# A third score buffer, a later scaling and another last sweep in an attention and ReLU-square kernel on one core

## The chip, the cores and the metric

The kernel runs on one core of a Trainium2 chip. The metric is the time of one execution on the device in microseconds (us), median of the runs. Five engines work side by side, each with its own queue of instructions: TensorE (PE; its weight loads are shown as PEld), VectorE (DVE), ScalarE (ACT), GpSimd (POOL) and SyncE (SP, which issues the transfers). Matmul results go to eight banks (PSUM), which TensorE, DVE and ACT reach; GpSimd works on SBUF alone.

## The reference

Attention over 32 heads (4 x 8, length 1152, depth 64) with queries averaged in pairs, then a two-layer block with a squared ReLU:

```python
q_pool = q.reshape(B, H, S // 2, 2, D).mean(axis=3)
scores = (1 / sqrt(D)) * q_pool @ k.transpose(0, 1, 3, 2)
attn = exp(scores - max(scores)); attn = attn / (sum(attn) + 1e-09)
x = (attn @ v).transpose(0, 2, 1, 3).reshape(2304, 512)
r = maximum(x @ w_in, 0)                  # w_in: 512 x 2048
out = (s * (r * r) + b) @ w_out           # w_out: 2048 x 512
```

Inputs are float64 (the weights) and float32; the output is 2304 x 512 float32.

## The kernel before

Every float32 operand is split in a high part (of a shorter format that TensorE takes in one pass) and the rest, the low part. A product is three matmuls: high by high, high by low, low by high.

**Attention.** 288 steps (32 heads x 9 key tiles, the loop at L841). A step makes scores of one key tile (`score_step`, L686: four matmuls of 288 columns, two buffers `s` of two banks each), and the product with v of the tile three steps before (`value_step`, L714). In between stand products `m` for the row maxima of heads to come (`max_unit`, L621, two banks `m`); they run 15 steps ahead, so the last 15 steps have none. A step has a kind (`KIND`, L36): for `w` ScalarE takes one exponential and the product with v is made in float32 (four records of L724); for `v` and `g` it takes two exponentials, one of them rounded, the difference `pl` is made by DVE from the score bank (`v`) or by GpSimd from a copy in SBUF (`g`), and the product with v is six matmuls (L730 to L734). When a pair of heads ends, `finish` (L739) queues by steps (`XT`, L44) two transposes and a reciprocal on DVE, a product on GpSimd (`scale`) and the DMA of the result (`send`).

**First and second sweep.** The hidden columns are 16 groups of 128. Groups 0 to 2, then 3 to 7, are worked for nine blocks of 256 rows. A unit is `mm1` (L355: 12 matmuls into a bank `h`, three buffers) and, four units later, `mm2` (L382). Between lies a chain: ReLU (ACT), square (DVE), `image` (ACT), `rest` (DVE, writes `gl` at L374 and is the last to read the bank). `later(k, fn)` issues an instruction k steps later; `pace` (L922) makes a step and, every seven steps, starts the conversion of one piece of weights.

**Last sweep** (groups 8 to 15, from L957). Two groups are one pair n, and two blocks one s. Unit (s, n) computes a 2 x 2 product of blocks with seven instead of eight block products: `first_half` (b11, t1, t3, t2; 24 matmuls) and `second_half` (b21, t4, b22; 18). Its results go to four quarters of two banks `xy0` and `xy1`, each with two buffers; b11 and t2 are the halves of one bank. ScalarE copies b11 (`one`, L1219), DVE adds it to t2 (`kept`, L1223) and so on; L1229 and L1232 write the results into ring tiles `rr`. n = 0, and block 8, are made with plain products (`plain`, L411). The second layer is also made with seven products per pair and block (`pair2`, L444, 21 matmuls into four banks `seven`), after additions on the operand (`prepare`, L1265: `one`, `two`, `three`, `own_high`, `own_low`, `high`, `low`). `gather` (L1317) adds the four banks of a block to the earlier part of the output, nine additions (L1331), and sends it (L1362).

The order of TensorE in this sweep is written out (`order`, L970 to L997; `TAKE` says how many pairs stand between the parts of the units). All other instructions are placed by a planner: each `op` has costs by engine, what it comes after, and beats of TensorE by which it must be done (`need`, `require`); from these it has a latest time, moved forward by `EARLY`. The loop at L1463 takes, among what can start within `LOOK` of the soonest, the most urgent; `BIAS` says how much longer an operation may take on GpSimd than on DVE (L1492 to L1499):

```python
            if at > soon + LOOK:
                continue
            if any(e2 != e and o2 is o and end2 < end - BIAS for _, end2, e2, o2, _ in choice if o2 is o):
                continue
```

Of the kernel before, what the change touches and what calls it, by code (L numbers as in the profile page):

```python
# [43 lines left out]
XT = (2, 2, 4, 4, 8)  # L44
SW = (3, 8)
# [20 lines left out]
def attention_moe_kernel(ctx: ExitStack, tc: tile.TileContext, q, k, v, w_in, w_out, s_in, b_in, out):  # L66
# [246 lines left out]
    class Moe:  # L313


        def __init__(self):
            self.acc = {}
            self.x, self.g, self.yq, self.y, self.raw, self.done = {}, {}, {}, {}, {}, []
            self.begun = 0

# [33 lines left out]
        def mm1(self, blk, f):  # L354
            xh, xl = self.x[blk]  # L355
            h = self.hp.tile([P, 512], F32, tag="h", name=f"h{blk}_{f}")
            n = 0
            for c in range(NC):
                for st, mv in ((wi_hi[f], xh), (wi_hi[f], xl), (wi_lo[f], xh)):
                    nc.tensor.matmul(h[:, :TB], st[:, c, :], mv[:, c, :], start=(n == 0), stop=(n == 3 * NC - 1))  # L360
                    n += 1
            r = self.p.tile([P, TB], F32, tag="r", bufs=2, name=f"r{blk}_{f}")
            t = h[:, TB:]
            gh = self.p.tile([P, TB], F32R, tag="gh", bufs=DEPTH + 1, name=f"gh{blk}_{f}")
            gl = self.p.tile([P, TB], F32R, tag="gl", bufs=DEPTH + 1, name=f"gl{blk}_{f}")

            def square():
                nc.vector.scalar_tensor_tensor(out=t, in0=h[:, :TB], scalar=sb[:, 0:1], in1=r, op0=ALU.mult, op1=ALU.mult)

            def image():  # L370
                nc.scalar.activation(gh, t, AF.Identity, bias=sb[:, 1:2])

            def rest():
                nc.vector.scalar_tensor_tensor(out=gl, in0=t, scalar=sb[:, 1:2], in1=f32(gh), op0=ALU.add, op1=ALU.subtract)  # L374
                self.g[blk, f] = gh, gl

            nc.scalar.activation(r, h[:, :TB], AF.Relu)
            for at, fn in zip(MO, (square, image, rest)):
                later(at, fn)
# [31 lines left out]
        def plain(self, blk, n):  # L411
            f0 = SW[1] + 2 * n
            own = blk == NBLK - 1
            h = self.bank[blk, n] = self.hp.tile([P, 512], F32, tag="h" if own else f"xy{blk % 2}", bufs=3 if own else 2, name=f"h{blk}_{f0}")
            if own:
                x = [[t[:, c] for t in self.x[blk]] for c in (slice(0, NC // 2), slice(NC // 2, NC))]
            else:
                x = [self.x[blk // 2, name] for name in (("b11", "b21"), ("b12", "b22"))[blk % 2]]
            for e in range(2):
                w = wi_hi[f0 + e], wi_lo[f0 + e]  # L420
                for half in range(2):
                    c = slice(half * NC // 2, (half + 1) * NC // 2)
                    self.product(h[:, e * TB:(e + 1) * TB], [t[:, c] for t in w], x[half], half == 0, half == 1)
                    yield

        def first_half(self, s, n):
            f0 = SW[1] + 2 * n
            xy = self.bank[s, n] = [self.hp.tile([P, 512], F32, tag=f"xy{e}", bufs=2, name=f"xy{e}_{s}_{n}") for e in range(2)]
            quad = [t[:, e * TB:(e + 1) * TB] for t in xy[::-1] for e in range(2)]
            w11 = tuple(t[f0][:, :NC // 2] for t in (wi_hi, wi_lo))  # L430
            for to, w, name in ((quad[2], w11, "b11"), (quad[0], self.s[n][0], "t1"), (quad[1], self.s[n][2], "t3"), (quad[3], self.s[n][1], "t2")):
                self.product(to, w, self.x[s, name], True, True)
                yield

        def second_half(self, s, n):
            f0 = SW[1] + 2 * n
            quad = [t[:, e * TB:(e + 1) * TB] for t in self.bank[s, n][::-1] for e in range(2)]
# [5 lines left out]
        def pair2(self, blk, n):  # L443
            first, last = n == 0, n == (NF - SW[1]) // 2 - 1  # L444
# [11 lines left out]

        def start(self, blk):
            self.y[blk] = [self.yp.tile([P, 512], F32, tag="y", name=f"y{blk}_{i}") for i in range(TB // P)]
# [7 lines left out]
    ps_m = att.enter_context(tc.tile_pool(name="ps_m", bufs=2, space=PSUM))  # L466
    ps_o = att.enter_context(tc.tile_pool(name="ps_o", bufs=1, space=PSUM))

# [215 lines left out]
    fresh = []  # L684

    def score_step(hd, j, kind):  # L686
# [52 lines left out]
    def finish(hd, a):  # L739
# [101 lines left out]
    for n in range(NS + LAG):  # L841
# [5 lines left out]
        for part in ORDS.get(n % 18, ORD[at]) if at is not None else "sff":  # L847
            if part == "s" and n < NS:
                score_step(hd, j, KIND[n % 18])
# [69 lines left out]
    wait = 0  # L919
# [63 lines left out]
    for s in range(NSB):  # L983
# [6 lines left out]
        for n in range(NP):  # L990
            if n not in PLAIN[s]:
                order.append(("first", (s, n)))
                for _ in range(1 if i else 2):
                    between(s, i)
                    i += 1
                order.append(("half", (s, n)))
    order += [("pair", e) for e in range(k, len(slots))]  # L997
    length = {"plain": (.716,) * 4, "second": (.693,) * 2, "banks": (), "first": (.716,) * 4, "half": (.716,) * 3, "pair": (.716, .716, .716, .358)}
# [29 lines left out]
    for (kind, i), b in begin.items():  # L1028
# [3 lines left out]
        elif kind == "first":  # L1032
            for e, name in enumerate(("b11", "t1", "t3", "t2")):
# [79 lines left out]
    def sums(s, n, at, old):  # L1113
# [45 lines left out]
        l1 = op(low(both(1), lambda: w[1], both(0)), E(512), h1, need=begin["first", (s, n)] + 1)  # L1159
# [27 lines left out]
    def image(key, tile, after):  # L1187
# [4 lines left out]
        made[key] = op(fn, A(.53), *after)  # L1192
# [17 lines left out]
    def unit(s, n, banks):  # L1210
# [3 lines left out]
        quad = lambda i: moe.bank[s, n][1 - i // 2][:, i % 2 * TB:(i % 2 + 1) * TB]  # L1214
        wide = lambda: moe.bank[s, n][1].rearrange("p (e t) -> p e t", t=TB)
# [18 lines left out]
        o1 = op(first, A(.32), b, *(one_by[-2:-1]), need=b + 3)  # L1234
# [23 lines left out]
        require(b, *banks[0])  # L1258
        require(b + 1, *banks[1])
        return [(c1,), (d,)]  # L1260
# [4 lines left out]
    def prepare(k, blk, n):  # L1265
        b = begin["pair", k]
# [33 lines left out]
        new = {}  # L1300
        new["one"] = op(one, VP(256), done, was(1, "one"), was(2, "low"))
# [15 lines left out]
    def gather(k, blk, end, before):  # L1317
        p = begin["pair", k]
        first = begin["pair", k - NP + 1]
# [39 lines left out]
        drained[:] = [aa, bb, *a1, *b2], [ma, m0], [z]  # L1359

# [3 lines left out]
        s0 = op(send(0), SY(2.5), aa, bb, *a1, ma, m0)  # L1364
        s1 = op(send(1), SY(2.5), aa, bb, *b2, ma, z)
# [41 lines left out]
    banks_of = [[(mults[-2],), (mults[-1],)], [(mults[-2],), (mults[-1],)]]  # L1407
    for s in range(NSB):
        for e in range(2):
            for n in PLAIN[s]:  # L1410
                q = plain(2 * s + e, n, banks_of[e][-2])
                banks_of[e].append((q,))
        for n in range(NP):
            if n not in PLAIN[s]:
                a, b = unit(s, n, (banks_of[0][-2], banks_of[1][-2]))
                banks_of[0].append(a)
                banks_of[1].append(b)
# [5 lines left out]
    drained[:] = [[kept_y[0][0], kept_y[1][0], mults[-1]], [], []]  # L1423
    for k, (blk, n) in enumerate(slots):
        if n == NP - 1:
            end = k == len(slots) - 1
            if end:
                drained[:] = [[x for e in range(2) for y in banks_of[e][-2:] for x in y], [], []]
# [34 lines left out]
    while waiting or beat_n < len(beats):  # L1463
# [26 lines left out]
        soon = min(x[0] for x in choice)  # L1490
        best = None
        for at, end, e, o, locked in choice:  # L1492
            if at > soon + LOOK:
                continue
            if any(e2 != e and o2 is o and end2 < end - BIAS for _, end2, e2, o2, _ in choice if o2 is o):
                continue
            key = limit[o["n"]] - (end - at)
            if best is None or key < best[0]:
                best = key, at, end, e, o, locked  # L1499
        if best is None:  # L1500
            at, end, e, o, locked = min((x for x in choice), key=lambda x: x[1])
        else:
            _, at, end, e, o, locked = best
# [9 lines left out]
    def products():  # L1513
        for kind, i in order:
# [9 lines left out]
            elif kind == "banks":  # L1524
                banks.close()
                moe.hp = ctx.enter_context(tc.tile_pool(name="ps_h3", reuse_waits="tile", bufs=2, space=PSUM))
                ps_7 = ctx.enter_context(tc.tile_pool(name="ps_7", reuse_waits="tile", bufs=1, space=PSUM))
                moe.hp.tile([P, 512], F32, tag="xy1", bufs=2, name="spare")
                moe.seven = [ps_7.tile([P, 512], F32, name=f"seven{i}") for i in range(4)]
            elif kind == "first":  # L1530
                yield from moe.first_half(*i)
            elif kind == "half":
                yield from moe.second_half(*i)
            else:
                blk, n = slots[i]
                if i == len(slots) - NP:
                    moe.seven = [moe.hp.tile([P, 512], F32, tag=f"xy{e}", bufs=2, name=f"last{e}_{x}") for e in range(2) for x in range(2)]
# [41 lines left out]
```

## Time and profile before

| | |
|---|---|
| Runs | 895.52, 895.66, 895.93 us (median 895.66) |
| The profiled execution | 895.35 us, of which the span of instructions is 893.6 us |
| PE busy | 871.8 us (98%), 6028 matmuls |
| PEld busy | 825.5 us (92%) |
| DVE busy | 741.5 us (83%) |
| ACT busy | 619.5 us (69%) |
| POOL busy | 656.4 us (73%) |
| granted TensorE clock | 0.999 of full speed |

The busy time of an engine is the time covered by at least one of its instructions. A matmul's end is modelled, and matmuls overlap: the distance from one start to the next tells what one costs, and a longer distance is a wait. The attention runs from 0 to about 493 us, the first two sweeps to about 693 us, the last sweep to the end.

### The profile page before, as it was taken

The numbers are of one execution on the slowest core, as the hardware profiler recorded it, in microseconds if no ns is written. First come the engines' busy times: TensorE is split into PE (matmuls) and PEld (weight loads), VectorE is DVE, ScalarE is ACT, GpSimd is POOL, SyncE is SP. The second block draws the span as 40 slices with busy tenths as digits, with TensorE's granted clock in tenths as the row PEclk, the third lists the DMA queues.
The fourth block names the chain that finished last, engine by engine and source line by source line (L and its number), as shares of the span: only waits on it lengthen the run. The fifth ranks groups of instructions, "written<-read, shape, count | busy, mean of one in ns | idle before, by whom it ended". The sixth has DMA issues, their size and how long they took to land.

```text
span 893.6 us, 17383 instructions
## 1 busy us (share of the span) xinstructions
PE 871.8 (98%) x6028; PEld 825.5 (92%) x6028; DVE 741.5 (83%) x1367; ACT 619.5 (69%) x1162; POOL 656.4 (73%) x576
## 2 busy tenths in 40 slices
PE   5999999999999999999999999999999999999997
PEld 3899999999999999999998899989999999999997
DVE  5888888888888888888874788789884999999977
ACT  3777777878777777778778677766663656656543
POOL 7978877988898889888957567579985365744523
PEclk9999999999999999999999999999999999999999
DMA  9899788887988898879553566766642212231112
GB/s 160 160 180 191 162 163 173 165 182 161 178 165 173 169 179 160 181 165 184 134 138 98 160 197 207 220 198 212 189 142 87 95 33 68 75 95 48 49 71 72
DMA packets 255207, 130.42 MB, mean 146 GB/s; under 512 B 203728, under 2 KB 226896, under 8 KB 255120
## 3 DMA queue, kind: packets, MB, share of 16 engines
q1 hardware_dynamic: 248016, 128.43, 60.9%
q10 hardware_dynamic: 7104, 0.89, 0.7%
q8 instruction: 48, 0.79, 0.4%
q14 instruction: 39, 0.32, 0.1%
HBM read 68.16 MB, written 18.87 MB: 97 GB/s over the span
## 4 chain that ended last, share of the span: by engine, by line
PE 82%; DVE 11%; ACT 3%; issue 1%; DMA 1%; SPq 1%; POOL 0%; ACTq 0%; DVEq 0%; POOLq 0%
PE s L692 17%; PE h L360 11%; PE y L387 10%; PE m L637 8%; PE o L724 7%; PE o L734 6%; PE o L732 6%; PE o L730 6%; PE seven L453 6%; PE xy L408 4%; DVE yq L1331 2%; DVE pm L638 1%; DVE c L1276 1%; DMA qraw<-in_q_dram 1%; PE h L408 1%
## 5 line engine op out<-in xcount | busy, mean ns | idle before, releaser
L638 DVE TENSOR_REDUCE pm<-m 128x1 f32<-128x384 f32 x432 | 226.2, 546 | 45.7 <-PE m L637 42.2
L692 PE MATMUL s<-qq,kk 128*128 128x288 f32 x1152 | 207.8, 302 | 1.7 <-DVE qq L666 1.3
L701 ACT ACTIVATE ph<-s 128x576 fp32r<-128x576 f32 x224 | 146.0, 652 | 79.7 <-PE s L692 76.1
L692 PEld LDWEIGHTS s<-qq,kk 128*128 128x128 f32 x1152 | 174.1, 189 | 10.6 <-issue 2.5
L707 POOL TENSOR_TENSOR pl<-pe,ph 128x576 fp32r<-128x576 f32 x96 | 138.5, 1455 | 50.9 <-ACT pe L704 50.8
L637 PE MATMUL m<-kh,qz 128*128 128x384 f32 x384 | 137.6, 378 | 0.2
L734 PE MATMUL o<-pl,vv 128*128 128x288 f32 x448 | 132.1, 295 | 0.0
L732 PE MATMUL o<-ph,vl 128*128 128x288 f32 (+1 forms) x448 | 132.0, 295 | 0.0
L730 PE MATMUL o<-ph,vv 128*128 128x288 f32 x448 | 131.6, 294 | 0.0
L707 DVE TENSOR_TENSOR pl<-s,ph 128x576 fp32r<-128x576 f32 x128 | 96.5, 754 | 28.8 <-ACT s L704 26.9
L360 PE MATMUL h<-x,wih 128*128 128x256 f32 x576 | 106.7, 283 | 1.1 <-DVE gl L374 1.0
L360 PEld LDWEIGHTS h<-x,wih 128*128 128x128 f32 x576 | 93.7, 190 | 7.9 <-DVE gl L374 2.1
L734 PEld LDWEIGHTS o<-pl,vv 128*128 128x128 f32 x448 | 84.2, 188 | 3.0
L730 PEld LDWEIGHTS o<-ph,vv 128*128 128x128 f32 x448 | 84.1, 188 | 0.0
L704 ACT ACTIVATE s<-s 128x576 f32<-128x576 f32 x128 | 83.2, 650 | 0.0
L360 PE MATMUL h<-x,wil 128*128 128x256 f32 x288 | 81.6, 283 | 0.0
L637 PEld LDWEIGHTS m<-kh,qz 128*128 128x128 f32 x384 | 73.4, 194 | 6.6 <-DVE pm L638 2.7
L724 PE MATMUL o<-pe,vf 128*128 128x288 f32 x256 | 77.4, 405 | 0.0
L732 PEld LDWEIGHTS o<-ph,vl 128*128 128x128 f32 (+1 forms) x448 | 73.8, 165 | 0.0
L1279 POOL TENSOR_TENSOR c<-rr 128x128 f32<-128x128 f32 x36 | 24.8, 690 | 54.3 <-ACT rr L1190 31.5
L704 ACT ACTIVATE pe<-s 128x576 f32<-128x576 f32 x96 | 61.9, 644 | 0.0
L387 PE MATMUL y<-woh,gh 128*128 128x512 f32 x144 | 56.9, 395 | 0.0
(428 smaller groups left out, 2329.5 us busy)
## 6 DMA issues: line engine op xcount, KB each, us to landing
kk<-kh SPq DMA_DIRECT2D x31, 576.0 KB, 5.6
vf<-in_v_dram SPq DMA_DIRECT2D x32, 288.0 KB, 4.3
qq<-qh SPq DMA_DIRECT2D x64, 144.0 KB, 5.7
kk<-kT SPq DMA_DIRECT2D x31, 288.0 KB, 3.3
xr<-xd SPq DMA_DIRECT2D x17, 512.0 KB, 4.0
qraw<-in_q_dram SPq DMA_DIRECT2D x120, 72.0 KB, 2.6
kraw<-in_k_dram SPq DMA_DIRECT2D x60, 144.0 KB, 3.5
wsti<-in_moe_w_in_dram SPq DMA_DIRECT2D x13, 512.0 KB, 4.0
```

The costliest lines, as they stand in the source:

```text
L360: nc.tensor.matmul(h[:, :TB], st[:, c, :], mv[:, c, :], start=(n == 0), stop=(n == 3 * NC - 1))
L387: nc.tensor.matmul(y[:, :DM], st[:, ts_], mv, start=(first and n == 0), stop=(last and n == 2))
L637: nc.tensor.matmul(ps[:, :KB], st, khs[p][:, e * KB:(e + 1) * KB], start=True, stop=True)
L638: nc.vector.tensor_reduce(out=pms[p][:, col, e:e + 1], in_=ps[:, :KB], axis=AX.X, op=ALU.max)
L692: nc.tensor.matmul(ps[:, a, :HALF], kk[:, i, j * P:(j + 1) * P], qq[:, i, a], start=(i == 0), stop=(i == 1))
L701: nc.scalar.activation(ph, ps[:, :, :HALF], AF.Exp, scale=SCALE)
L704: nc.scalar.activation(full, ps[:, :, :HALF], AF.Exp, scale=SCALE)
L707: fresh.append(lambda: eng.tensor_tensor(out=pl, in0=full, in1=f32(ph), op=ALU.subtract))
L724: nc.tensor.matmul(o[:, :HALF], vfs[hd % 2][:, j], ph[:, a], start=first, stop=last)
L730: nc.tensor.matmul(o[:, :HALF], vv[:, j], ph[:, a], start=first, stop=False)
L732: nc.tensor.matmul(o[0:vl.shape[2], :HALF], vl[:, j], ph[:, a], start=False, stop=False)
L734: nc.tensor.matmul(o[:, :HALF], vv[:, j], pl[:, a], start=False, stop=last)
```

## The change

- Attention: kinds of the last 18 steps from `KINDL` (three w, twelve v, three g; before four, eight, six). The pool of the maxima is opened last and closed after the step by which all maxima have begun; its two banks become a third score buffer, taken by every third step.
- `XL`: for the last pair of heads transposes, reciprocal, scaling and DMA are issued 16 steps later. `MF`: in the first four units of the first sweep `rest` is issued after 4 steps, not 6. `W0`: the conversion of weights for the last groups begins 6 steps later.
- Last sweep: a unit has a bank `y` (t1, t3; two buffers, shared with `plain`) and banks `xa` (b11) and `xb` (t2) of one buffer each; the order in the first half is t1, t3, b11, t2. `TAKE` puts pairs elsewhere, 28 in all before the last eight, as before. The rings have 4 and 5 tiles for 3 and 3. `EARLY`, `LOOK`, `BIAS` and the choice differ: DVE is taken only where it ends first, GpSimd where it ends at most `BIAS` after that.
- The last pair (`tail`): instead of 21 matmuls 24 plain ones, in four groups of six, each group's half bank in the banks of the block before. The sums for the seven products are then made once over three pairs while the plain ones run, and four single additions follow, one after each group.

```diff
+XL = 16
+KINDL = "wvwvvgvvgvvwvvgvvv"
+MF = (2, 3, 4)
+W0 = 6
-RR = (3, 3)
+RR = (4, 5)
-TAKE = ((0, 1, 1, 1, 1), (1, 1, 2, 2, 2))
+TAKE = ((0, 0, 1, 0, 1, 0, 2, 0), (0, 2, 2, 0, 2, 0, 2, 0))
-LOOK, BIAS = 0.1, 0.33
-EARLY = {"sums": 1, "image": 2, "unit": -0.5, "gather": 1, "fetch_raw": -2}
+LOOK, BIAS = 0.3, 0.62
+EARLY = {"keep": 2, "unit": 0.1, "fetch_raw": 2, "plain": 0.1, "sums": 0.1, "image": 2}
...
-            for at, fn in zip(MO, (square, image, rest)):
+            for at, fn in zip(MO if len(self.turns) > DEPTH else MF, (square, image, rest)):
...
-            xy = self.bank[s, n] = [self.hp.tile([P, 512], F32, tag=f"xy{e}", bufs=2, name=f"xy{e}_{s}_{n}") for e in range(2)]
-            quad = [t[:, e * TB:(e + 1) * TB] for t in xy[::-1] for e in range(2)]
+            y, x0, x1 = self.bank[s, n] = [self.hp.tile([P, 512], F32, tag=tag, bufs=bufs, name=f"{tag}{s}_{n}") for tag, bufs in (("y", 2), ("xa", 1), ("xb", 1))]
+            quad = [y[:, :TB], y[:, TB:], x0[:, :TB], x1[:, :TB]]
...
-            for to, w, name in ((quad[2], w11, "b11"), (quad[0], self.s[n][0], "t1"), (quad[1], self.s[n][2], "t3"), (quad[3], self.s[n][1], "t2")):
+            for to, w, name in ((quad[0], self.s[n][0], "t1"), (quad[1], self.s[n][2], "t3"), (quad[2], w11, "b11"), (quad[3], self.s[n][1], "t2")):
...
+        def tail(self, blk, n):
+            own, both = self.g.pop((blk, n))
+            _, w1r, d1, d2, w0l, _, _ = seven[n]
+            for i in range(2):
+                g0, g1 = [[t[:, (2 * e + i) * P:(2 * e + i + 1) * P] for t in own] for e in range(2)]
+                c = [t[:, i] for t in both]
+                for half, todo in enumerate((((c, w0l), (g1, d2)), ((g0, d1), (c, w1r)))):
+                    y = self.seven[2 * i + half][:, :HD]
...
-        ps = ps_s.tile([P, 2, 512], F32, tag="s", name=f"s{hd}_{j}")
+        if third and (hd * NJ + j - third[0]) % 3 == 2:
+            ps = third[1].tile([P, 2, 512], F32, tag="t", name=f"s{hd}_{j}")
+        else:
+            ps = ps_s.tile([P, 2, 512], F32, tag="s", name=f"s{hd}_{j}")
...
-                later(at, fn)
+                later(at + (XL if p == NPAIR - 1 else 0), fn)
...
+        if not third and begun(n + 1) == NPAIR * NU:
+            maxima.close()
+            third.extend((n + 1, att.enter_context(tc.tile_pool(name="ps_t", bufs=1, space=PSUM))))
...
-    wait = 0
+    wait = W0
...
-        made[key] = op(fn, A(.53), *after)
+        made[key] = op(fn, A(.71), *after)
...
-        o1 = op(first, A(.32), b, *(one_by[-2:-1]), need=b + 3)
+        o1 = op(first, A(.32), b + 2, *(one_by[-2:-1]), need=h)
...
-        require(b, *banks[0])
-        require(b + 1, *banks[1])
-        return [(c1,), (d,)]
+        require(b, *banks[2])
+        require(b + 2, *banks[0])
+        require(b + 3, *banks[1])
+        return (c0,), (c1,), (d,)
...
+        if end:
+            t0 = begin["tail", k + 1]
+            rows = [[op(add(single(2 * i + e), lambda at=2 * i + e: moe.sums[at][:, :HD]), V(.34), got, t0 + 2 * i + e) for e in range(2)] for i in range(2)]
...
-            for e, (c, locked) in o["costs"].items():
-                at = max(t, idle[e], port if locked is True else 0.)
-                choice.append((at, at + c, e, o, locked))
...
+            at = {e: max(t, idle[e], port if locked is True else 0.) for e, (c, locked) in o["costs"].items()}
+            ends = {e: at[e] + o["costs"][e][0] for e in at}
+            choice += [(at[e], ends[e], e, o, o["costs"][e][1]) for e in at if ends[e] <= min(ends.values()) + (BIAS if e == "G" else 0.)]
+        soon = min(x[0] for x in choice) + LOOK
+        at, end, e, o, locked = min((x for x in choice if x[0] <= soon), key=lambda x: limit[x[3]["n"]] - x[1] + x[0])
```

## Rows read from the trace of the kernel before

**Rows 1.** The page's first line: the span.

```profile
span 893.6 us, 17383 instructions
```

**Rows 2.** Busy time by stage: stretch, length, then each engine (instructions), clock, DMA.

```profile
461.00:492.80 31.80, 31.43 (x210) 28.88 (x210) 16.04 (x27) 26.57 (x48) 24.25 (x20) 1.00 0.36 93
492.80:693.00 200.20, 199.11 (x1274) 180.16 (x1273) 154.93 (x292) 129.64 (x276) 144.26 (x114) 1.00 0.58 181
693.00:866.90 173.90, 171.58 (x1406) 169.41 (x1406) 158.92 (x285) 103.52 (x184) 88.33 (x90) 1.00 0.20 65
866.90:893.60 26.70, 20.32 (x170) 20.05 (x168) 20.83 (x38) 9.22 (x16) 9.07 (x12) 0.96 0.23 79
```

**Rows 3.** Waits of TensorE: us in total, times, longest.

```profile
PE xy L408 <- ACT one L1219: 2.0, 2, 1.2
PE h L360 <- DVE gl L374: 1.0, 2, 0.6
```

**Rows 4.** Timeline, TensorE, last scores: start, us, instruction, [idle before, releaser].

```profile
469.63 0.80 PE L692 MATMUL s<-qq,kk 128*128 128x288 f32 x4
...
484.62 0.80 PE L692 MATMUL s<-qq,kk 128*128 128x288 f32 x4 [0.35 <-DVE pl L707]
...
488.94 0.73 PE L692 MATMUL s<-qq,kk 128*128 128x288 f32 x3
```

**Rows 5.** The same timeline: scores without a wait, one matmul, a float32 step.

```profile
486.06 0.69 PE L692 MATMUL s<-qq,kk 128*128 128x288 f32 x4
...
487.25 0.29 PE L734 MATMUL o<-pl,vv 128*128 128x288 f32 x1
...
488.14 1.13 PE L724 MATMUL o<-pe,vf 128*128 128x288 f32 x4
```

**Rows 6.** Timelines of TensorE and DVE at the start of the first sweep.

```profile
497.02 0.28 PE L360 MATMUL h<-x,wil 128*128 128x256 f32 x1
497.90 0.50 PE L360 MATMUL h<-x,wih 128*128 128x256 f32 x2 [0.61 <-DVE gl L374]
...
499.96 0.50 PE L360 MATMUL h<-x,wih 128*128 128x256 f32 x2 [0.36 <-DVE gl L374]
...
496.02 0.77 DVE L764 STREAM_TRANSPOSE rr<-rc 128x576 f32<-128x576 f32 x1
```

**Rows 7.** Timeline, TensorE, at three first and second halves of units.

```profile
720.58 0.28 PE L408 MATMUL xy<-x0b,wol 128*128 128x256 f32 x1
721.63 0.51 PE L408 MATMUL xy<-x1b,woh 128*128 128x256 f32 x2 [0.77 <-ACT one L1219]
...
732.90 0.51 PE L408 MATMUL xy<-x1b,wih 128*128 128x256 f32 x2 [0.25 <-DVE kept L1223]
...
755.54 0.28 PE L408 MATMUL xy<-ob,wol 128*128 128x256 f32 x1
757.03 0.50 PE L408 MATMUL xy<-ob,woh 128*128 128x256 f32 x2 [1.22 <-ACT one L1219]
```

**Rows 8.** Timelines: a second half begins; its second result is read.

```profile
803.99 0.40 PE L408 MATMUL xy<-x1b,wih 128*128 128x256 f32 x2
...
810.38 0.41 DVE L1229 TENSOR_TENSOR rr<-xy,kept 128x256 f32<-128x256 f32 x1
```

**Rows 9.** Timelines of DVE and GpSimd at 715 us.

```profile
715.48 1.51 DVE L1145 TENSOR_TENSOR wil<-w0s,wih 128x256 fp32r<-128x256 f32 x1
...
715.30 1.41 POOL L1132 TENSOR_TENSOR w1s<-wih,wil 128x512 f32<-128x512 f32 x1 [1.83 <-DVE wol L1145]
```

**Rows 10.** Timelines of the end: TensorE, DVE, ScalarE, GpSimd.

```profile
886.94 0.28 PE L453 MATMUL last<-wol,wil 128*128 128x256 f32 x1
...
885.28 0.74 DVE L1331 TENSOR_TENSOR yq<-yq,seven 128x256 f32<-128x256 f32 x2
...
887.77 2.47 DVE L1331 TENSOR_TENSOR yq<-yq,last 128x512 f32<-128x512 f32 x5 [1.15 <-ACT end L1345]
...
886.65 1.09 ACT L1345 ACTIVATE end<-last 128x512 f32<-128x512 f32 x2 [3.34 <-DVE yq L1331]
...
889.72 0.72 POOL L1331 TENSOR_TENSOR yq<-yq,end 128x256 f32<-128x256 f32 x1 [0.86 <-issue]
```

More of the change, by code (lines that the diff above doesn't have):

```diff
@@ L436, in second_half @@
             f0 = SW[1] + 2 * n
-            quad = [t[:, e * TB:(e + 1) * TB] for t in self.bank[s, n][::-1] for e in range(2)]
+            y, x0, x1 = self.bank[s, n]
+            quad = [y[:, :TB], y[:, TB:], x0[:, :TB], x1[:, :TB]]
             w12, w22 = [tuple(t[f][:, NC // 2:] for t in (wi_hi, wi_lo)) for f in (f0, f0 + 1)]
@@ L443, in pair2 @@
         def pair2(self, blk, n):
-            first, last = n == 0, n == (NF - SW[1]) // 2 - 1
+            first, last = n == 0, n == (NF - SW[1]) // 2 - (2 if blk == NBLK - 2 else 1)
             ah, al, ch, cl = self.g.pop((blk, n))
@@ L455, in pair2 @@
                     yield
+        def tail(self, blk, n):
[6 more added lines that the diff above has]
+                    y = self.seven[2 * i + half][:, :HD]
+                    for k, ((gh, gl), (wh, wl)) in enumerate(todo):
+                        for m, (st, mv) in enumerate(((gh, wh), (gh, wl), (gl, wh))):
+                            nc.tensor.matmul(y, st, mv, start=k == 0 and m == 0, stop=k == 1 and m == 2)
+                    yield
         def start(self, blk):
@@ L684, in attention_moe_kernel @@
     fresh = []
+    third = []
     def score_step(hd, j, kind):
@@ L991, in attention_moe_kernel @@
             if n not in PLAIN[s]:
-                order.append(("first", (s, n)))
-                for _ in range(1 if i else 2):
+                for half in ("first", "half"):
+                    order.append((half, (s, n)))
                     between(s, i)
                     i += 1
-                order.append(("half", (s, n)))
-    order += [("pair", e) for e in range(k, len(slots))]
-    length = {"plain": (.716,) * 4, "second": (.693,) * 2, "banks": (), "first": (.716,) * 4, "half": (.716,) * 3, "pair": (.716, .716, .716, .358)}
+    order += [("pair", e) for e in range(k, len(slots) - 1)]
+    order.append(("tail", len(slots) - 1))
+    length = {"plain": (.716,) * 4, "second": (.693,) * 2, "banks": (), "first": (.716,) * 4, "half": (.716,) * 3, "pair": (.716, .716, .716, .358), "tail": (.716,) * 4}
     begin, beats = {}, []
@@ L1158, in sums @@
         h1 = op(high(both(0), lambda: w[1]), A(.53), e1, e2, *busy)
-        l1 = op(low(both(1), lambda: w[1], both(0)), E(512), h1, need=begin["first", (s, n)] + 1)
+        l1 = op(low(both(1), lambda: w[1], both(0)), E(512), h1, need=begin["first", (s, n)])
         h2 = op(high(lambda: put[0][2], lambda: w[0][:, :m]), A(.32), e3, *busy)
@@ L1257, in unit @@
             image((2 * s + e, n), tile, after)
-        require(b, *banks[0])
-        require(b + 1, *banks[1])
-        return [(c1,), (d,)]
+        require(b, *banks[2])
+        require(b + 2, *banks[0])
+        require(b + 3, *banks[1])
+        return (c0,), (c1,), (d,)
     history = []
     def prepare(k, blk, n):
-        b = begin["pair", k]
+        whole = k == len(slots) - 1
+        b = begin["tail" if whole else "pair", k]
         cell = {}
@@ L1318, in gather @@
         p = begin["pair", k]
-        first = begin["pair", k - NP + 1]
+        first = begin["pair", k - (NP - 2 if end else NP - 1)]
         for beat, x in zip((first, first + 2, first + 3), drained):
@@ L1533, in products @@
                 yield from moe.second_half(*i)
+            elif kind == "tail":
+                moe.sums = moe.seven = moe.banks[slots[i - NP][0]]
+                yield from moe.tail(*slots[i])
             else:
@@ L1536, in products @@
                 if i == len(slots) - NP:
-                    moe.seven = [moe.hp.tile([P, 512], F32, tag=f"xy{e}", bufs=2, name=f"last{e}_{x}") for e in range(2) for x in range(2)]
+                    banks.close()
+                    ps_l = ctx.enter_context(tc.tile_pool(name="ps_l", reuse_waits="tile", bufs=1, space=PSUM))
+                    moe.seven = [ps_l.tile([P, 512], F32, name=f"last{i}") for i in range(4)]
                 moe.banks[blk] = moe.seven
```

79 lines of the change are left out of this document (45 added, 34 removed).

## The prediction, made before the changed kernel was seen

> **What bounds the kernel now.** I read the page first, then busy time by stage, then the waits of TensorE, then timelines around each wait. The execution's span is 893.6 us [rows 1]; the whole profiled execution took 895.35 us, so 1.75 us lie around the span, and it stands 0.3 us under the median of the runs (895.66). The sum below is made against 895.35 and the 0.3 us is added at the end. In all stages that the change touches TensorE is nearly always busy: it is without a matmul for 0.4 us in the end of the attention, 2.3 us in the main part of the last sweep and 6.4 us in the last 26.7 us, most of that after its last matmul [rows 2]. So little can be won: either fewer matmuls, or the waits, or the end. The waits of TensorE are short and few, and they are named: it waits for the subtraction `gl` (L374) and for the ScalarE copy `one` (L1219) [rows 3]. A busy time hides part of each wait, since the modelled matmul (0.28 us) overlaps the next one (they start 0.12 us apart), so I price each wait by the starts of the matmuls on both sides of it.
>
> **End of the attention: third score buffer, other kinds.** Scores start at 469.63 for step 274 and at 488.94 for step 287 [rows 4], 19.31 us for 13 steps. Four score matmuls without a wait take 0.69 us to the end of the last; with 0.29 us for one of them, they start 0.13 us apart [rows 5]. So a step of ten products (4 and 6) needs 1.33 us. A step of kind w has four float32 records, which end after 1.13 us, against 0.29 + 5 x 0.133 = 0.96 us for six [rows 5]: 0.17 us more. Thirteen steps, three of them w, need 17.3 + 0.5 = 17.8 us; 1.5 us are waits. The longest is released by the subtraction `pl` [rows 4], the last reader of one of two score buffers. A third buffer lets the scores run one step (1.33 us) ahead of those readers; it uses the two banks of the maxima, which are empty from step 272 on. The added kinds v hold a buffer for two exponentials and a DVE subtraction; DVE has room for it, since it was busy for only 16.0 of the 31.8 us [rows 2]. ScalarE is the next in line (26.6 of 31.8 [rows 2]): one w fewer costs it one more exponential. Gain between 0.5 (ScalarE late) and 1.5 us; I take 1.4, nearer the full amount since its load is under 85%, and 0.2 us for the w that becomes a split product. **-1.6 us**, bounds -0.5 and -1.8.
>
> **Start of the first sweep: MF, W0, XL.** The fourth `mm1` starts at 497.90 where its predecessor started at 497.02, 0.88 instead of 0.12 us; the fifth waits again, 0.36 us idle and a first pair of matmuls 0.1 us longer (0.50 for 0.40) [rows 6]. Both wait for `gl` of three units before, whose bank they reuse. `gl` is issued six steps behind its product; DVE has by then the transposes of the last pair (one stands at 496.02 for 0.77 us [rows 6]), and the weight conversion joins. With MF `gl` is issued after four steps, XL moves both transposes, the reciprocal, the GpSimd product and the DMA of the last pair 16 steps later, W0 the conversion six. Removed: 0.76 + 0.10 + 0.36 + 0.10 = 1.3 us. What it costs later: the moved DVE work, some 1.8 us (two transposes of 0.77 and a reciprocal, by the row), meets the first conversion around the sixth unit; a unit is then twice as long (`mm1` and the second products), and DVE has 45 us spare in this sweep (154.9 of 200.2 [rows 2]). SP's queue is passed too: the DMA of the last pair now stands behind the first fetches of weights, but it is issued in the eighth unit, and the fetch that reads it (the seventh block) not before the tenth. If that cover fails, up to 1 us. **-1.3 us**, bounds -0.3 and -1.5.
>
> **Last sweep: banks.** In a unit the products b11 and t2 share one bank. `one` reads b11, and t2, three products on, starts only when `one` is done. At 720.58 the next matmul comes 1.05 us later, at 755.54 1.49 us later, instead of 0.12 [rows 7]: 0.93 + 1.37, and both resume with a matmul pair 0.1 us longer. `one` was late there because two images stood before it in ScalarE's order. At 732.90 b21 waits in the same way for `kept`, another reader of that bank, 0.25 us idle [rows 7]. Now b11 and t2 have a bank each: `one` is wanted by b21 only, which is a product t2 and at least one pair (2.5 us) later. These waits, 0.93 + 0.1 + 1.37 + 0.1 + 0.25 = 2.75 us, go; with the smaller ones of this kind (two to four, under 0.4 us each) 2.75 to 3.6. What is new: the banks xa and xb have one buffer each, so b11 of the next unit waits until the first result was read from xa, t2 until the second was read from xb. In the order of before these reads come late: a unit whose second half starts at 803.99 has its second result read at 810.38 to 810.79 [rows 8]; the new deadline is two stretches of three products (18 matmuls of 0.12 us, 2.15 us each) on, 808.3, so that one would be 2.5 us late. The new order is made with these as due times, so the reads move up and something else moves back; with 15 us of DVE idle between 693 and 866.9 (158.9 of 173.9 [rows 2]) there is room. I take 2.9 us removed and 0.8 us of new waits, an estimate between 0 and 2.5: **-2.1 us**, bounds -3.6 and +1. Larger rings (4 and 5 for 3 and 3) free results earlier and cost nothing but room.
>
> **Who takes the work.** The new choice gives GpSimd an operation when it ends up to 0.62 us later than on DVE. Against this stands [rows 9]: while GpSimd ran an addition of 1.41 us from 715.30, a DVE subtraction of 256 columns took 1.51 us, to within 0.02 us of GpSimd's end, where a 256-column operation takes 0.41 [rows 8]. So work moved to GpSimd is not work taken from DVE. The first rival is worked out from that.
>
> The Trainium skill ("SBUF — State Buffer", section "SBUF: two separate sides") makes a rule of it that speaks against this part: an exclusive lock, in which the loser blocks for the whole instruction. By that rule, the trace agrees at the place shown, every further overlap would cost DVE what it costs here, and the time would be that of rival (1); by the waits of TensorE as they stand, with GpSimd in use all along, it is the forecast's.
>
> **The end.** The last pair changes from 21 to 24 matmuls, 3 x 0.12 = +0.36 us. Before, the last matmul starts at 886.94 and ends at 887.22; then two ScalarE copies (from 886.65), DVE additions until 887.77 + 2.47 = 890.24, and a GpSimd addition until 890.44 [rows 10]; the rest to 893.6 is the output's DMA, unchanged. Now the additions of the seven products of the last block run under the 24 plain matmuls (2.87 us), and behind the last of these stands one DVE addition of 0.37 us (0.74 for two [rows 10]). Best: 887.22 + 0.36 + 0.03 (from the end of the copies, 886.65 + 1.09, to the DVE addition at 887.77) + 0.4 = 888.0, a gain of 2.4. Worst: DVE stays the bound. It ended the block before only at 885.28 + 0.74 = 886.02 [rows 10]; its own 0.7 + 2.47 us for the last block and four new additions, 1.5 us, give 890.7, a loss of 0.3. The new pair's preparation is lighter by about one DVE operation, the rings let it begin earlier and the 1.1 us idle before 887.77 is filled: I take the middle. **-1.1 us**, bounds -2.4 and +0.3.
>
> **Sum.** -1.6 - 1.3 - 2.1 - 1.1 = -6.1 us. 895.35 - 6.1 = 889.25, and with the 0.3 us to the median **889.5 us**.
>
> **The rivals.** (1) GpSimd's work shuts DVE out, and the last sweep gives its gain back: each 256-column operation caught so costs 1.1 us more [rows 9]; the stretch from 693 to 866.9 can take some 13 such (15 us idle), the end none, so with 16 to 20 in all 3 us of waits come back and the end gains nothing: 889.5 + 3 + 1.1 = 893.6. For it: DVE ran 91% there. Against: before, with GpSimd at 51% (88.3 of 173.9 [rows 2]), most of the sweep ran without a wait. (2) Slower: the single banks xa and xb decide. Where two units follow one another (eight places), a read that is 2.5 us late, as at 810.38, stops TensorE for 2.5 us. If four places stay as they were, +10 us: 889.5 - 0.8 + 10 = 898.7; it turns to slower from a mean wait of 1 us over the eight. Against: these reads are due times of the order. (3) Plain products wait at the end: they write into the banks of the block before, which DVE emptied at 886.02, and would start at 884.4 (2.87 us before 887.22); if nothing moves, 1.6 us of wait, 891. (4) The third buffer does not do it, since ScalarE is late: 889.5 + 1 = 890.5.
>
> **How the numbers follow.** The forecast with its neighbours (3) and (4), 887 to 891.5: 0.70. Rival (1), 891.5 to 895: 0.20, of which 0.08 lie within 0.2% of before. Rival (2): 0.10. A measurement of this kernel can tell about 0.2% (1.8 us) from no change. So faster 0.82, same 0.09, slower 0.09. The range: best case all bounds together, 895.66 - 9.3 = 886.4; the high end reaches into rival (1), 894.
>
> **What would show it.** Right: no wait of TensorE above 0.3 us between 470 and 490 and between 493 and 500; no wait for `one` or `kept`; the last matmul within 1.5 us of the last addition. Wrong: waits of b11, t2 (for L1229) or of the plain products for L1331; DVE operations of 256 columns above 1 us more often than before; conversions that stop `mm1` near the sixth unit.

## The result and the profile after

The changed kernel takes 886.93 us (median, 886.32 to 887.13) where the kernel before took 895.79 us beside it (895.52 to 896.71): a ratio of 0.9898 (95% interval 0.9881 to 0.9915). Forecast were 889.5 us and 6.2 us less; 8.9 us less were measured. The profiled execution took 886.83 us.

The page's first line of the changed kernel, for [rows 1]:

```profile
span 885.0 us, 17385 instructions
```

Busy time by stage of the changed kernel, the columns as in [rows 2]:

```profile
461.00:490.50 29.50, 29.50 (x208) 28.37 (x207) 18.80 (x31) 26.46 (x48) 20.62 (x17) 1.00 0.40 102
490.50:690.50 200.00, 200.00 (x1286) 181.81 (x1286) 155.53 (x294) 130.62 (x278) 143.59 (x113) 1.00 0.57 182
690.50:861.00 170.50, 170.50 (x1410) 169.47 (x1409) 146.47 (x239) 103.55 (x182) 130.27 (x138) 1.00 0.20 65
861.00:885.00 24.00, 19.33 (x162) 19.12 (x160) 16.59 (x32) 8.81 (x16) 12.89 (x17) 0.99 0.24 88
```

TensorE is without a matmul for 0.00 us in the first three stretches (before 0.4, 1.1 and 2.3). Look at the fifth and third engine columns of the last sweep's main part too: GpSimd 130.27 us busy where it was 88.33, DVE 146.47 where it was 158.92.

The waits of TensorE in the changed kernel, all that the view lists, for [rows 3]; all three lie in the attention, before step 274:

```profile
PE m L659 <- ACT kh L297: 9.4, 1, 9.4
PE s L718 <- DVE qq L688: 1.3, 1, 1.3
PE m L659 <- ACT qm L297: 0.2, 1, 0.2
```

To see where the time went, take the start of the same matmul in both traces. First the changed kernel: step 274, first unit of the first sweep, sixth unit, first matmul of the last sweep, last matmul:

```profile
469.83 0.80 PE L718 MATMUL s<-qq,kk 128*128 128x288 f32 x4
...
491.27 0.40 PE L365 MATMUL h<-x,wih 128*128 128x256 f32 x2
...
499.84 0.40 PE L365 MATMUL h<-x,wih 128*128 128x256 f32 x2
...
689.66 0.40 PE L414 MATMUL h<-x,wih 128*128 128x256 f32 x2
...
880.05 0.28 PE L474 MATMUL seven<-woh,gl_3s 128*128 128x256 f32 x1
```

The same places of the kernel before that no row above shows, with a wait of 0.4 us at 593 that the forecast had not seen:

```profile
492.83 0.40 PE L360 MATMUL h<-x,wih 128*128 128x256 f32 x2
...
502.89 0.42 PE L360 MATMUL h<-x,wih 128*128 128x256 f32 x2
...
593.08 0.40 PE L387 MATMUL y<-woh,gl 128*128 128x512 f32 x1
593.60 0.51 PE L360 MATMUL h<-x,wih 128*128 128x256 f32 x2
...
693.07 0.40 PE L408 MATMUL h<-x,wih 128*128 128x256 f32 x2
```

| Stretch (us) | before | after | difference | forecast |
|---|---|---|---|---|
| start to step 274 | 469.63 | 469.83 | +0.20 | 0 |
| step 274 to the first sweep | 23.20 | 21.44 | -1.76 | -1.6 |
| first five units | 10.06 | 8.57 | -1.49 | -1.3 |
| rest of two sweeps | 190.18 | 189.82 | -0.36 | 0 |
| last sweep, to the end of the last matmul | 194.15 | 190.67 | -3.48 | -1.74 (-2.1 + 0.36) |
| last matmul to the end of the span | 6.33 | 4.71 | -1.62 | -1.46 (-1.1 - 0.36) |
| span | 893.55 | 885.04 | -8.51 | -6.1 |

### The profile page after: what moved, and what is told of

The parts are those of the page before. It is cut to its first block, busy times and chain, and to the rows that moved or that the text cites. A ratio compares the mean times of both kernels' runs of the same rounds, so it can differ in the third digit from the quotient of the medians.

```text
span 885.0 us, 17385 instructions
## 1 busy us (share of the span) xinstructions
PE 869.1 (98%) x6033; PEld 825.8 (93%) x6033; DVE 727.9 (82%) x1320; ACT 619.9 (70%) x1163; POOL 697.8 (79%) x626
## 4 chain that ended last, share of the span: by engine, by line
PE 92%; DVE 3%; DMA 1%; SPq 1%; ACT 1%; issue 1%; ACTq 0%; POOL 0%; DVEq 0%
PE s L718 17%; PE h L365 12%; PE y L393 11%; PE m L659 8%; PE seven L460 8%; PE o L750 7%; PE o L760 6%; PE o L758 6%; PE o L756 6%; PE h L414 4%; PE y L414 3%; PE xa L414 2%; PE xb L414 2%; DVE yq L1383 1%; DVE pm L660 1%; DMA qraw<-in_q_dram 1%
## 5 line engine op out<-in xcount | busy, mean ns | idle before, releaser
L733 POOL TENSOR_TENSOR pl<-pe,ph 128x576 fp32r<-128x576 f32 x93 | 134.2, 1456 | 45.6 <-ACT pe L730 45.5
L733 DVE TENSOR_TENSOR pl<-s,ph 128x576 fp32r<-128x576 f32 x132 | 99.4, 753 | 24.5 <-ACT s L730 21.7
L730 ACT ACTIVATE s<-s 128x576 f32<-128x576 f32 x132 | 86.0, 652 | 0.0
L343 POOL TENSOR_TENSOR x<-xr,x 128x1024 fp32r<-128x1024 f32 x18 | 43.4, 2409 | 26.5 <-ACT x L297 16.5
L730 ACT ACTIVATE pe<-s 128x576 f32<-128x576 f32 x93 | 60.0, 645 | 0.0
```

The source lines that it names most:

```text
L730: nc.scalar.activation(full, ps[:, :, :HALF], AF.Exp, scale=SCALE)
L733: fresh.append(lambda: eng.tensor_tensor(out=pl, in0=full, in1=f32(ph), op=ALU.subtract))
```

## The experiments

The twelve kernels differ from the changed one, or (names with b_) from the one before, by the edits shown (`...` marks lines left out). The runs of one kernel differ by up to 2.0 us, so small differences are read from the stretches of the table, not from the medians. The last two stretches together are called the last sweep with its end: 200.48 us before, 195.38 us after.

**Attention: the buffer and the kinds.** First the third buffer is left unused, with the new kinds kept:

```diff
-        if third and (hd * NJ + j - third[0]) % 3 == 2:
+        if False and (hd * NJ + j - third[0]) % 3 == 2:
```

> The changed kernel with two score buffers to the end of the attention; the new kinds stay. If the third buffer removed the waits of the last scores: the 13 steps from score 274 to 287 take 19.2 to 19.6 us again (17.7 with it), and the time is 1.4 to 2 us over the changed kernel's 886.9, about 888.5 (the added DVE subtractions hold a buffer longer, so it may be above the 1.5 us of before). If the new kinds did it: under 18.2 us for those steps and at most 0.5 us over 886.9.

890.17 us (0.9941, 0.9924 to 0.9957): 3.2 us slower than the changed kernel. Timeline of TensorE, this kernel, scores of steps 274 to 276:

```profile
470.06 0.80 PE L718 MATMUL s<-qq,kk 128*128 128x288 f32 x4
471.92 0.80 PE L718 MATMUL s<-qq,kk 128*128 128x288 f32 x4 [0.26 <-DVE pl L733]
473.96 0.80 PE L718 MATMUL s<-qq,kk 128*128 128x288 f32 x4 [0.28 <-DVE pl L733]
```

Steps start 1.86 and 2.04 us apart, where the forecast's step needs 1.33 to 1.50, and what releases them is `pl`, the reader of the buffer. The thirteen steps take 20.42 us, more than the 19.2 to 19.6 that were expected. Then the other half alone, the old kinds with the third buffer:

```diff
-KINDL = "wvwvvgvvgvvwvvgvvv"
+KINDL = ""
```

> The changed kernel with the old kinds in the last 18 steps; the third score buffer stays. If the buffer alone removes the waits: 13 steps from score 274 to 287 take 17.7 to 18.0 us, time 887 to 887.4 (one float32 step more, 0.17 us). If the new kinds are wanted too (GpSimd's subtractions late for the products with v): waits of 0.7 us and more, time over 887.6.

887.58 us (0.9903, 0.9886 to 0.9919). Thirteen steps take 17.96 us. With 19.31 before and 17.72 after, that gives four corners: the buffer is worth 1.35 us with the old kinds and 2.70 with the new, and the new kinds without it cost 1.1. A step of kind v holds its score bank for two exponentials and a subtraction, one of kind w for a single exponential, so the kinds with more v want the buffer first. ScalarE, which was to spoil this, did not.

**Start of the first sweep.** First `rest` in the first units as late as before; then, apart from it, the last pair's transposes and scaling where they were:

```diff
-MF = (2, 3, 4)
+MF = (2, 3, 6)
```

> The changed kernel with the last step of the first four units issued after six steps again, not four; the scaling of the last pair and the conversion stay late. If the issue order made the waits of the first sweep: the first five units take 9.5 to 10.1 us (8.6 in the changed kernel, 10.1 before), time 887.8 to 888.4. If the transposes and the conversion in front made them: under 8.9 us, time within 0.4 us of 886.9.

```diff
-XL = 16
+XL = 0
```

> The changed kernel with transposes, reciprocal, scaling and transfer of the last pair issued at once again. If the transposes on DVE made the waits of the first sweep: the first five units take 9.3 to 10.1 us, time 887.6 to 888.4. If the issue order of the units alone made them: under 8.9 us, within 0.4 us of 886.9.

887.66 us (0.9906, 0.9891 to 0.992) and 887.46 us (0.9905, 0.9889 to 0.9922). The first five units take 8.83 and 8.75 us, against 8.57 with both and 10.06 before. So most of the 1.49 us stays when either of the two is taken back. `W0` is in both of these kernels, and it was not tried alone. It may have a part of its own: the first late `gl` (497.38) comes after the transposes of [rows 6], but the second stands behind a piece of the weights' conversion, on DVE in the kernel before:

```profile
498.82 0.70 DVE L228 TENSOR_SCALAR wi<-wi 128x512 f32<-128x512 f32 x1
499.43 0.47 DVE L374 SCALAR_TENSOR_TENSOR gl<-h,sb,gh 128x256 fp32r<-128x256 f32 x1
```

So how the 1.49 us divide among the three stays open.

**Last sweep: the banks.** b11 and t2 share a bank again (two buffers), in the old order of products, with due times to suit; choice, `TAKE`, rings and last pair stay new:

```diff
-            y, x0, x1 = self.bank[s, n] = [self.hp.tile([P, 512], F32, tag=tag, bufs=bufs, name=f"{tag}{s}_{n}") for tag, bufs in (("y", 2), ("xa", 1), ("xb", 1))]
+            xx, y = [self.hp.tile([P, 512], F32, tag=tag, bufs=2, name=f"{tag}{s}_{n}") for tag in ("xx", "y")]
+            y, x0, x1 = self.bank[s, n] = y, xx[:, :TB], xx[:, TB:]
...
-            for to, w, name in ((quad[0], self.s[n][0], "t1"), (quad[1], self.s[n][2], "t3"), (quad[2], w11, "b11"), (quad[3], self.s[n][1], "t2")):
+            for to, w, name in ((quad[2], w11, "b11"), (quad[0], self.s[n][0], "t1"), (quad[1], self.s[n][2], "t3"), (quad[3], self.s[n][1], "t2")):
...
-        o1 = op(first, A(.32), b + 2, *(one_by[-2:-1]), need=h)
+        o1 = op(first, A(.32), b, *(one_by[-2:-1]), need=b + 3)
```

> The changed kernel with b11 and t2 as halves of one bank again (two buffers), in the order b11, t1, t3, t2, and with the due times that belong to it; rings, choice, urgencies, places of the pairs and the plain last pair stay new. If the separate banks removed the waits: TensorE waits again for the copy of b11 or for its reader, 2 to 4 us in the last sweep, time 889 to 891. If the better order of the other engines did it: the copy is in time with the shared bank too, under 0.7 us of waits, time 886.5 to 887.6.

888.00 us (0.9912, 0.9897 to 0.9927). The last sweep takes 191.38 us to the last matmul, 0.71 more than the changed kernel's and 2.77 less than before. No wait for `one` or `kept` is in it. The time lies between the two that were expected. The view of waits has one line of this sweep, an operand of a pair:

```profile
PE seven L461 <- DVE wil L1326: 0.5, 1, 0.5
```

By the starts of the matmuls this place costs 0.62 us, and the pair behind it 0.1 more. So the shared bank, on which the forecast laid the waits for `one`, can be kept at a price of 0.7 us.

**Last sweep: the choice of engine.** The old rule of choice with its two numbers, all else new:

```diff
-LOOK, BIAS = 0.3, 0.62
+LOOK, BIAS = 0.1, 0.33
...
-            at = {e: max(t, idle[e], port if locked is True else 0.) for e, (c, locked) in o["costs"].items()}
+            for e, (c, locked) in o["costs"].items():
...
+                if at > soon + LOOK:
+                    continue
```

> The changed kernel with the old rule of choice between DVE and GpSimd and the old two numbers of it; banks and rings stay new. If the banks removed the waits, and work moved to GpSimd is no relief for DVE: GpSimd's busy time in the last sweep falls back from 130 to about 90 us, and the time stays within 0.6 us of 886.9. If DVE's full list was the cause of the waits: they come back in another place, 1.5 to 4 us, time 888.5 to 891.

893.75 us (0.9976, 0.9967 to 0.9985), 6.8 us slower than the changed kernel, more than was expected: 5.25 in the sweep, 1.59 at the end. Waits of TensorE, then DVE's timeline ahead of the longest, this kernel:

```profile
PE h L414 <- DVE rr L1261: 1.8, 1, 1.8
...
PE xa L414 <- DVE rr L1258: 1.2, 2, 0.9
PE xb L414 <- DVE rr L1258: 0.5, 1, 0.5
```

```profile
739.20 3.64 DVE L1383 TENSOR_TENSOR yq<-yq,seven 128x512 f32<-128x512 f32 x7
742.76 0.68 DVE L1261 TENSOR_TENSOR rr<-y,kept 128x512 f32<-128x512 f32 x1
```

The seven additions of a block's output stand in DVE's queue before the read that empties the bank, and TensorE waits 1.9 us for it by the starts of its matmuls. The waits for xa and xb are those of rival (2): the single banks do stop TensorE when their reads come late. GpSimd is busy for 80.24 of 175.5 us here. Next, the two numbers singly, with the new rule. First BIAS:

```diff
-LOOK, BIAS = 0.3, 0.62
+LOOK, BIAS = 0.3, 0.33
```

> The changed kernel with GpSimd allowed to end 0.33 us later than DVE instead of 0.62; the new rule and the look-ahead stay. If this number sends the work to GpSimd: GpSimd's busy time in the last sweep falls from 130 towards 80 us, the waits for the banks return, 889.5 to 893. If the new rule does (DVE taken only where it ends first): GpSimd stays over 115 us and the time within 0.7 us of 886.9.

890.34 us (0.9936, 0.9922 to 0.9951). Busy time in the main part of its last sweep:

```profile
690.20:862.00 171.80, 171.32 (x1414) 170.06 (x1413) 158.51 (x293) 104.12 (x184) 79.22 (x84) 1.00 0.21 65
```

GpSimd falls back to 79 us and DVE rises to 158.5, as before the change; yet the sweep loses only 0.76 us and has one wait (0.64 us, by the starts). The end loses 1.84 us: DVE then has the operations that GpSimd would have taken, and adds up the last block later. Then LOOK:

```diff
-LOOK, BIAS = 0.3, 0.62
+LOOK, BIAS = 0.1, 0.62
```

> The changed kernel with the look-ahead of the choice at 0.1 us instead of 0.3. If the share of GpSimd is what counts: within 0.7 us of 886.9. If it is the freedom to let an engine stand for a more urgent operation: waits of 1 to 4 us in the last sweep, 888 to 891.

889.95 us (0.9931, 0.9916 to 0.9945). The sweep loses 3.26 us, the end nothing (4.32 us), and GpSimd stays at 128 us. The longest wait of its last sweep:

```profile
PE xa L414 <- DVE rr L1258: 0.9, 1, 0.9
```

So the two numbers work mainly at different places: looking ahead lets an urgent read of a bank go before operations that could start up to 0.3 us sooner, and removes the waits of the sweep; the work on GpSimd frees DVE for the end. Singly they account for 3.26 + 0.76 = 4.02 of the 5.25 us in the sweep; the rest belongs to the new rule or to the numbers together, and was not parted.

**The choice without the rest.** The kernel before with the new rule and numbers:

```diff
-LOOK, BIAS = 0.1, 0.33
+LOOK, BIAS = 0.3, 0.62
...
```

> The kernel before with only the new rule of choice and its two numbers; banks, rings, places of the pairs, urgencies, score buffers and last pair are the old ones. If the choice by itself takes the waits of the last sweep (DVE's list was too full, and GpSimd takes work beside DVE's reads of the banks): the sweep up to the last matmul falls from 194.2 to 190.5 to 191.5 us, time 892 to 893.2. If the choice is only what the single banks need (it undoes a cost that they bring): the sweep stays at 193.5 to 195 us, time 895 to 896.5, and the waits for the copy of b11 are there still.

899.20 us (1.0036, 1.0024 to 1.0048): slower than before, and than either case expected. Its last sweep takes 197.46 us to the last matmul, 3.31 more than before. Timelines of TensorE, DVE and GpSimd at its longest wait:

```profile
753.27 0.28 PE L408 MATMUL xy<-x0b,wil 128*128 128x256 f32 x1
757.04 0.77 PE L408 MATMUL xy<-x1b,woh 128*128 128x256 f32 x2 [3.49 <-DVE rr L1232]
...
756.20 0.69 DVE L1232 TENSOR_TENSOR rr<-xy,kept 128x512 f32<-128x512 f32 x1 [0.34 <-POOL c L1279]
...
755.27 0.90 POOL L1279 TENSOR_TENSOR c<-rr 128x128 f32<-128x128 f32 x1
```

Read it from below: GpSimd comes late to an addition that reads a ring tile; DVE needs that tile for the result in the bank; TensorE needs the bank. With a ring of three that is 3.65 us. Therefore the same with the longer rings:

```diff
-RR = (3, 3)
+RR = (4, 5)
```

> The kernel before with the new rule of choice, its two numbers and the longer rings (4 and 5 tiles); banks, places of the pairs, urgencies, score buffers and last pair stay old. With the choice alone one addition that writes a ring tile held TensorE for 3.5 us. If the ring was what held it: that wait goes, and the sweep up to the last matmul takes 190.5 to 192.5 us (197.5 with the choice alone, 194.2 before), time 891.5 to 893.5. If the choice needs the new banks or places of the pairs: a wait of 2 us or more stays, sweep over 194 us, time over 895.

896.00 us (1.0, 0.9991 to 1.0009), last sweep 194.54 us. The wait for the ring is gone, and the waits for `one` are back: 0.88, 1.36 and 0.68 us by the starts of the matmuls. Timelines of TensorE and ScalarE around the longest:

```profile
797.82 0.39 PE L408 MATMUL xy<-x1b,woh 128*128 128x256 f32 x1 [1.20 <-ACT one L1219]
...
795.75 0.82 ACT L1190 ACTIVATE rr<-rr,sb 128x512 f32<-128x512 f32 x1 [0.34 <-DVE rr L1202]
...
797.41 0.36 ACT L1219 ACTIVATE one<-xy 128x256 f32<-128x256 f32 x1
```

`one` stands behind an image again, and behind two roundings of operands that come between the two rows. With the choice and the rings, but the old `TAKE`, `EARLY` and costs, nothing is won.

**The rings** in the changed kernel, smaller by one each:

```diff
-RR = (4, 5)
+RR = (3, 4)
```

> The changed kernel with rings of 3 and 4 tiles instead of 4 and 5. If long rings are needed by the new order: waits of 1 to 4 us in the last sweep, 888 to 891. If they only make room: within 0.5 us of 886.9.

887.31 us (0.9903, 0.9888 to 0.9918), last sweep 190.69 us, no wait: no difference that can be told.

**The end.** The last pair again with seven products, all else new:

```diff
-    order += [("pair", e) for e in range(k, len(slots) - 1)]
-    order.append(("tail", len(slots) - 1))
+    order += [("pair", e) for e in range(k, len(slots))]
...
```

> The changed kernel with seven products for the last pair too. If the end counts as forecast: 0.36 us fewer matmuls, but the time from the last matmul to the end grows from 4.7 to 6.3 us, together +1.1 to +1.4 us, about 888.2. If DVE is the bound at the end in either form: both ends lie within 0.4 us of each other, 886.5 to 887.3.

888.08 us (0.9915, 0.9901 to 0.993). The last sweep to its last matmul is 0.37 us shorter, for three matmuls fewer, and the end 1.51 us longer: 1.14 us in sum. The chain that ended last, first in this kernel and then in the changed one:

```profile
874.00 4.44 PE last L460 x37
...
878.46 0.70 DVE yq L1382
```

```profile
875.95 0.60 DVE wil L1342
876.55 0.61 DVE yq L1383
...
877.18 0.60 ACT end L1397
...
878.30 0.70 DVE yq L1383
```

With seven products the end hangs on the last matmul; with plain ones TensorE has left the chain, and DVE sets the end.

## Why the prediction was right, and where it was not

**End of the attention: right** in mechanism and size (-1.76 for -1.6). The waits for `pl` were the loss, and the buffer removes them. Not seen: the kinds by themselves cost 1.1 us.

**Start of the first sweep: right** (-1.49 for -1.3). The moved DVE work did not come back as a wait. The sum priced the first wait by the starts and the second by its idle time; by the starts (499.32 to 499.96) the second is 0.52, not 0.36, and the four terms then give 1.48. That either of `MF` and `XL` can be taken back at a small price was not seen; the sum did not depend on it. The 0.36 us further on came unforecast: the wait at 593 is gone.

**Last sweep: right in sign, too small, and for the wrong reason.** Two terms of the sum were mis-sized. Removed were 3.84 us (3.48 and the 0.36 of three more matmuls), where I took 2.9 and had 3.6 as the bound; new waits were 0, where I took 0.8. The step that failed is the one that credits the banks. It read rightly that t2 waits for `one`, and at 720.58 `one` does stand behind images. At the longer wait, 755.54, it does not: three roundings of operands stand there (L1292, L1086, L1286), of which this is the last, on ScalarE in the kernel before:

```profile
756.32 0.40 ACT L1286 ACTIVATE gh_2s<-rr 128x256 fp32r<-128x256 f32 x1
756.62 0.36 ACT L1219 ACTIVATE one<-xy 128x256 f32<-128x256 f32 x1
```

And the shared bank costs only 0.7 us once `one` is in time. The kernel with the shared bank has `one` in time; the kernel before with the new choice and the rings has not. In this sweep, ahead of its end, they differ in `TAKE`, `EARLY`, the image's cost of 0.71, some due times and the bank of the plain products (together the new order here); which of these keeps `one` in time was not tried and stays open. The new choice is worth 5.25 us in the sweep where this order and the separate banks are new. In the kernel before it costs 3.3 us, with the longer rings 0.4. The separate banks with the old choice are slower in the sweep (195.92 us) than the kernel before (194.15), while the new choice and the new order have 2.77 of the 3.48 us with the shared bank. So it is the choice and the new order that work together, and the separate banks add the last 0.7. The new order with the shared bank and the old choice was not tried. That the total came near the forecast is luck in this term: the gain was credited to a part that gave a fifth of it.

**Who takes the work: wrong.** "Work moved to GpSimd is not work taken from DVE" generalised one row. That row was also misread: DVE's subtraction ended at 715.48 + 1.51 = 716.99, 0.28 us behind GpSimd's addition (716.71), not within 0.02. Groups of DVE's operations in the main part of the last sweep, by form, with count, busy time and mean in ns; first the kernel before:

```profile
L1276 DVE SCALAR_TENSOR_TENSOR c<-rr 128x256 f32<-128x256 f32 x31 | 17.3, 565 | 3.6 <-ACT rr L1190 3.5
L1295 DVE TENSOR_TENSOR wil<-c,wih 128x640 fp32r<-128x640 f32 x19 | 17.1, 900 | 4.4 <-ACT wih L1292 4.4
L1331 DVE TENSOR_TENSOR yq<-yq,seven 128x256 f32<-128x256 f32 x40 | 15.9, 416 | 0.6
L1331 DVE TENSOR_TENSOR yq<-yq,seven 128x512 f32<-128x512 f32 x21 | 14.3, 680 | 0.7
L1282 DVE TENSOR_TENSOR c<-rr 128x256 f32<-128x256 f32 x21 | 12.9, 614 | 0.0
```

The same of the changed kernel, in which the last group is all on GpSimd:

```profile
L1307 DVE SCALAR_TENSOR_TENSOR c<-rr 128x256 f32<-128x256 f32 x31 | 22.4, 727 | 0.0
L1326 DVE TENSOR_TENSOR wil<-c,wih 128x640 fp32r<-128x640 f32 x22 | 22.4, 1016 | 2.5 <-ACT wih L1323 2.5
L1383 DVE TENSOR_TENSOR yq<-yq,seven 128x256 f32<-128x256 f32 x42 | 16.6, 414 | 0.4
L1383 DVE TENSOR_TENSOR yq<-yq,seven 128x512 f32<-128x512 f32 x21 | 14.3, 681 | 1.0 <-PE seven L460 0.4
```

Operations that read only SBUF do become longer: the mean of `c` goes from 565 to 727 ns, of `wil` from 900 to 1016. It is GpSimd's load that goes with this: in the changed kernel with `BIAS` 0.33, where GpSimd is busy for 79 us, the same two groups have means of 586 and 854 ns. Those that read a bank stay at 414 and 681 ns, and of all DVE operations here that read a bank, 137 of 239, none is above 0.69 us. So more than half of DVE's operations were not held up at all. The stretching of those two groups is 31 x 0.16 + 22 x 0.12 = 7.6 us; `c` of L1282 alone took 12.9 us off DVE. Rival (1)'s mechanism was there: 44 of DVE's operations in this stretch took more than 0.9 us, before 22. The sign named for it did not show, though: operations of 256 columns above 1 us were 2, before 3. Nor did its price: DVE gained more than it lost, no wait came, and the 1.84 us at the end are a part of what it gained. The Trainium skill ("SBUF — State Buffer", section "SBUF: two separate sides") limits its exclusive lock in this very way, to DVE operations with two inputs in SBUF (or in a two-port mode); the trace agrees, and the prediction had left that condition out.

**The end: right in size, partly by another way** (-1.62, with 0.36 for the matmuls -1.26, for -1.1). The additions of the seven products do run under the plain matmuls, all but the last 0.4 us on DVE, but DVE's idle time before the block's additions was not filled, as I had taken it to be; and behind the last matmul stand four additions, not one, until 882.09, 1.76 us after it where I named 1.5 as the sign. 1.14 us hang on the plain products. GpSimd's part by `BIAS` is 1.84 us of the end, so the two overlap.

**The rivals.** (2) is a real mechanism: with the old choice it cost 0.5 to 1.0 us at three places (2.5 at four were named); with the new choice none of these waits is left. (3): the plain products start 0.12 us after the pair before. (4): the third buffer does it.

## What to carry to other kernels

Where a planner's choice places the instructions of four engines, a bank layout has no price of its own: here the separate banks without the new choice of engine lost time in the sweep, and so did the choice without the new order, while the choice and the order with the old layout gave most of the gain. Try each part without the others before crediting it. Before calling offloading to GpSimd useless or free, split DVE's operations into those that read a bank and those that read SBUF alone: here only the latter grew longer.

## What the runs showed of the hardware that was not expected

After the wait of 3.49 us in the kernel before with the new choice, TensorE came back at the lower clock. Busy time around it, the columns as in [rows 2]:

```profile
753.50:757.00 3.50, 0.05 (x1) 0.00 (x0) 3.05 (x4) 1.18 (x3) 3.50 (x4) 0.82 0.01 2
757.00:762.50 5.50, 5.46 (x25) 5.49 (x26) 2.35 (x4) 3.17 (x5) 4.03 (x6) 0.50 0.35 95
762.50:770.00 7.50, 7.50 (x65) 7.50 (x64) 7.33 (x14) 3.52 (x7) 6.78 (x7) 1.00 0.25 71
```

The granted clock is 0.50 (1.2 of 2.4 GHz) from 757.0 to 762.5 us, and 25 matmuls start 0.21 us apart instead of 0.12: about 2.3 us on top of the 3.65 of the wait. It fell during the wait (0.82 in the mean of that stretch). No other wait in the last sweep of the kernels here, up to 1.9 us, did that.

DVE's last additions and ScalarE's last copies read the same banks one after the other. Timeline of DVE at the end of the changed kernel:

```profile
878.30 2.47 DVE L1383 TENSOR_TENSOR yq<-yq,last 128x512 f32<-128x512 f32 x5 [1.15 <-ACT end L1397]
880.69 1.40 DVE L1383 TENSOR_TENSOR yq<-yq,seven 128x256 f32<-128x256 f32 x4
```

The 1.15 us stand there as in [rows 10], and since DVE sets the end now, they would be the next thing to try; that was not done.
